# Key sums of linear attention turned round on column tiles, with GpSimd summing z and new constants for the kernel's planner

## The chip, the cores and the metric

The kernel runs on one NeuronCore of a Trainium2 chip. The metric is the device time of one execution in microseconds (us); lower is better. The names of the engines in the profile are PE (TensorE, matmuls), PEld (its weight loads), DVE (VectorE), ACT (ScalarE), POOL (GpSimd) and SP (the engine that issues nearly all DMAs).

## The reference

Random-feature attention over 8 batches, 8 heads, 576 positions and 64 dimensions, followed by a two-layer feed-forward block with softplus on the 4608 tokens:

```python
def phi(x):
    proj = np.einsum('bhsd,md->bhsm', x, omega)
    sq = np.sum(x * x, axis=-1, keepdims=True) / 2.0
    h = proj - sq
    h = h - np.max(h, axis=-1, keepdims=True)
    return np.exp(h) / np.sqrt(m)
q_p, k_p = (phi(q_s), phi(k_s))
kv = np.einsum('bhsm,bhsd->bhmd', k_p, v)
z = np.sum(k_p, axis=2)
num = np.einsum('bhsm,bhmd->bhsd', q_p, kv)
den = np.einsum('bhsm,bhm->bhs', q_p, z)[..., None] + 1e-06
x = (num / den)                # tokens x 512
h = x @ w_in                   # 512 x 2048
g = np.maximum(h, 0.0) + np.log1p(np.exp(-np.abs(h)))
out = g @ w_out                # 2048 x 512
```

There are 128 features. All is float32; the feed-forward products are made of three fp32r products each (high x high, high x low, low x high).

## The kernel before

**Units.** Attention is worked in *quads*: four heads of one batch, two quads a batch, 16 in all. A quad has five units `u` for keys (tile names in `k`) and five for queries (`q`): four of 128 positions and a last one with the remaining 64. A unit is loaded, its squares are summed, its rows are projected on omega (`project`, line 445 for batches 0 and 1, line 588 from batch 2 on), and the features are the exponentials (`ph`), 128 of them for four heads side by side. Batch 0 ("early") has its own path.

**Key sums.** For keys of batch 1 on, `plan_sums` makes kv and z on TensorE: `outer` (line 676) multiplies features (weights, 128 positions x 128 features) by V with a 65th column of ones (128 x 65, 4 heads one after the other), so column 64 of each head is z. Units 0 to 2 go into one sum, units 3 and 4 into a second; `part` (ScalarE) keeps the first aside in `kvp`, `whole` (VectorE) adds the second to it and gives `kvs`; `z`, `z_turn`, `out_z` and `in_z` turn z by a VectorE transpose, send it out in 4 stores and read it back broadcast to all partitions (`zb`). Query features are divided by their denominator (VectorE reduction `den`, line 784; the division itself mostly on GpSimd, line 794), turned through DRAM (`qdq`) and multiplied by `kvs` (`num`, lines 954, 997 and 1048), which gives the columns of x. There the weights are 128 x 64, so the two heads of a pair stand in two column tiles of the array, side by side.

**Feed-forward.** Blocks of 512 tokens (the first two of 256) run through 16 slices of 128 hidden units: `layer1` (lines 1412 to 1414), softplus on ScalarE and VectorE, `layer2` (lines 1441 to 1443). The last two blocks are joined in `plan_pair` (lines 1199 and 1256 to 1258), seven products in place of eight. Each weight slice is 512 KB, packed, and is opened by five steps in `plan_weights`: lowest bits (line 333 on ScalarE, 335 on VectorE), `rebias`, `joined`, `high_part`, `low_part`.

**What sets the order.** Each piece of work is a `Work` with a due time and a cost for each engine that can do it. `in_order` plays these through and takes, on the engine that is free first, the startable work that is due first; the program is written out in that order, and every engine runs its instructions in it. Costs (`act`, `dve`, `pool`, `dma` and numbers beside each `do`) and due times (offsets from `due`, and the tables `KEYS`, `QUERIES`, `IN`, `OUT`) are constants. `with_fill` puts matmuls of no use ("fillers", line 1571, weights `ident` or `idle`) where the play leaves TensorE idle in its first part, to keep its clock up. Work that uses the port shared by VectorE and GpSimd is kept apart by added waits.

## Time and profile before

| what | value |
|---|---|
| three runs, median | 996.35 us (996.18 to 997.45) |
| span of the profiled execution | 995.2 us |
| TensorE busy | 989.6 us (99%) |
| VectorE, ScalarE, GpSimd busy | 783.6, 722.7, 206.4 us |
| granted TensorE clock, mean | 1.000 |
| transfers, whole span | 124.49 MB, 125 GB/s |

The span goes from the first to the last instruction of the profiled execution; the runs' own times lie 1.15 us above it in the median. A busy TensorE in this table is one on which some matmul is in flight; matmuls overlap, so the price of one is read from the starts of its neighbours, not from its duration. An fp32 product shows as two records, an fp32r product or a transpose as one.

### The profile page before, as it was taken

What the parts mean: (1) busy time and instruction counts of PE and PEld (TensorE: products, weight loads), DVE (VectorE), ACT (ScalarE), POOL (GpSimd) and SP (SyncE); (2) the same over time, 40 slices, a digit from 0 to 9 for tenths busy, and PEclk for the clock granted to TensorE, in tenths of its full rate; (3) what the DMA queues carried; (4) which work ended last, traced back from release to release, by engine and by line L of the source; (5) the groups of instructions that cost most, each with busy time, mean ns of one, the idle gap of its engine ahead of it and who ended that gap; (6) DMA issues with size and microseconds to landing.
All of it is one profiled execution on the core that took longest, in us unless ns stands there. A gap on an engine that the chain in (4) does not pass through costs nothing.

```text
span 995.2 us, 17488 instructions
## 1 busy us (share of the span) xinstructions
PE 989.6 (99%) x5495; PEld 830.9 (83%) x5495; DVE 783.6 (79%) x2306; ACT 722.7 (73%) x1794; POOL 206.4 (21%) x235
## 2 busy tenths in 40 slices
PE   9999999999999999999999999999999999999998
PEld 8988888888888888888878888888888878888886
DVE  6899986889898888888879886887787958676620
ACT  7999887879777777877777776776776656666520
POOL 3313232312221122101212121112011214223000
PEclk9999999999999999999999999999999999999999
DMA  9982355454464455543454444434542331000011
GB/s 321 352 282 90 111 162 152 138 160 141 136 183 139 125 138 160 159 128 113 138 144 133 123 129 119 155 106 113 138 141 75 80 92 43 0 1 1 1 43 42
DMA packets 117628, 124.49 MB, mean 125 GB/s; under 512 B 16288, under 2 KB 93728, under 8 KB 117536
## 3 DMA queue, kind: packets, MB, share of 16 engines
q1 hardware_dynamic: 117392, 123.26, 41.4%
q8 instruction: 43, 0.70, 0.3%
q14 instruction: 49, 0.40, 0.1%
q10 hardware_dynamic: 144, 0.13, 0.0%
HBM read 97.37 MB, written 25.98 MB: 124 GB/s over the span
## 4 chain that ended last, share of the span: by engine, by line
PE 98%; DVE 1%; ACT 0%; issue 0%
PE banks L1441 11%; PE banks L1412 11%; PE banks L1442 10%; PE banks L1443 10%; PE banks L1413 10%; PE banks L1414 10%; PE banks L1199 8%; PE banks L676 5%; PE banks L588 5%; PE banks L1256 3%; PE banks L1258 3%; PE banks L1257 3%; PE banks L445 2%; PE banks L997 2%; PE banks L735 1%; PE banks L954 1%
## 5 line engine op out<-in xcount | busy, mean ns | idle before, releaser
L1412 PE MATMUL banks<-xh,wi 128*128 128x512 f32 (+1 forms) x512 | 188.8, 369 | 0.4 <-DVE u L1427 0.4
L1413 PE MATMUL banks<-xl,wi 128*128 128x512 f32 (+1 forms) x512 | 186.1, 363 | 0.0
L1414 PE MATMUL banks<-xh,wi 128*128 128x512 f32 (+1 forms) x512 | 185.9, 363 | 0.0
L1441 PE MATMUL banks<-wo,gh 128*128 128x512 f32 x448 | 178.6, 399 | 0.0
L1442 PE MATMUL banks<-wo,gh 128*128 128x512 f32 x448 | 175.5, 392 | 0.0
L1443 PE MATMUL banks<-wo,gl 128*128 128x512 f32 x448 | 175.0, 391 | 0.0
L1418 ACT ACTIVATE u<-banks 128x512 f32<-128x512 f32 (+1 forms) x128 | 70.1, 548 | 73.4 <-PE banks L1414 60.5
L1412 PEld LDWEIGHTS banks<-xh,wi 128*128 128x128 f32 x512 | 96.4, 188 | 17.2 <-issue 1.2
L1414 PEld LDWEIGHTS banks<-xh,wi 128*128 128x128 f32 x512 | 96.4, 188 | 15.6
L1413 PEld LDWEIGHTS banks<-xl,wi 128*128 128x128 f32 x512 | 96.6, 189 | 13.9
L1441 PEld LDWEIGHTS banks<-wo,gh 128*128 128x128 f32 x448 | 84.2, 188 | 18.5 <-issue 4.3
L1443 PEld LDWEIGHTS banks<-wo,gl 128*128 128x128 f32 x448 | 84.1, 188 | 18.5
L1442 PEld LDWEIGHTS banks<-wo,gh 128*128 128x128 f32 x448 | 84.4, 188 | 13.3
L1427 DVE SCALAR_TENSOR_TENSOR u<-banks,u 128x512 f32<-128x512 f32 (+1 forms) x128 | 78.4, 613 | 15.8 <-ACT u L1424 15.4
L612 ACT ACTIVATE phq<-phq,smq 128x128 f32<-128x128 f32 x216 | 71.8, 395 | 14.7 <-DVE smq L608 14.7
L794 POOL TENSOR_TENSOR phq<-phq,dnq 128x512 f32<-128x512 f32 (+1 forms) x46 | 41.9, 911 | 189.2 <-DVE dnq L790 113.1
L612 ACT ACTIVATE phk<-phk,smk 128x128 f32<-128x128 f32 x216 | 71.9, 397 | 10.7 <-DVE smk L608 10.7
L784 DVE CUSTOM_DVE_ANT_0 restq<-phq,zb 128x128 f32<-128x128 f32 x280 | 72.7, 293 | 4.8 <-ACT phq L612 4.0
L1421 ACT ACTIVATE u<-u 128x512 f32<-128x512 f32 (+1 forms) x128 | 74.4, 581 | 1.8
L1424 ACT ACTIVATE u<-u 128x512 f32<-128x512 f32 (+1 forms) x128 | 74.6, 584 | 1.3
L1431 ACT CAST gh<-u 128x512 fp32r<-128x512 f32 (+1 forms) x97 | 55.8, 576 | 18.0 <-PE banks L1442 17.1
L1435 POOL TENSOR_TENSOR gl<-u,gh 128x512 fp32r<-128x512 f32 (+1 forms) x41 | 45.1, 1101 | 106.4 <-ACT gh L1431 31.5
(224 smaller groups left out, 2097.3 us busy)
## 6 DMA issues: line engine op xcount, KB each, us to landing
xk<-ky SPq DMA_DIRECT2D x48, 384.0 KB
xq<-qy SPq DMA_DIRECT2D x48, 384.0 KB
qdq<-restq SPq DMA_DIRECT2D x56, 256.0 KB
out<-o SPq DMA_DIRECT2D x36, 256.0 KB
vk<-vv SPq DMA_DIRECT2D x70, 130.0 KB
rawi<-wi SPq DMA_DIRECT2D x16, 512.0 KB
rawo<-wo SPq DMA_DIRECT2D x16, 512.0 KB
q<-qdq SPq DMA_DIRECT2D x64, 128.0 KB
```

The source lines that it names most:

```text
L612: nc.scalar.activation(b["ph"][:, c], b["ph"][:, c], AF.Exp, bias=b["sm"][:, 2, c : c + 1])
L784: i = nc.vector.tensor_tensor_reduce(jk[r, c], ph[r, c], q.zb[r, h], 1.0, 1e-6, ALU.mult, ALU.add, dn[r, 0, c : c + 1])
L1199: nc.tensor.matmul(b[key], x, y, start=fresh and not kk and not n, stop=kk == 1 and n == 2, skip_group_check=True)
L1412: nc.tensor.matmul(b["h"], wh, xh[:, cc, t], start=cc == 0, stop=False)
L1413: nc.tensor.matmul(b["h"], wh, xl[:, cc, t], start=False, stop=False)
L1414: nc.tensor.matmul(b["h"], wl, xh[:, cc, t], start=False, stop=cc == NCC - 1)
L1421: nc.scalar.activation(b["u"], b["u"], AF.Exp, scale=-1.0)
L1424: nc.scalar.activation(b["u"], b["u"], AF.Ln, bias=1.0)
L1427: nc.vector.scalar_tensor_tensor(b["u"], b["h"], 0.0, b["u"], ALU.max, ALU.add)
L1441: nc.tensor.matmul(acc[tt], gh, w2[fc][:, 0], start=fc == 0, stop=False)
L1442: nc.tensor.matmul(acc[tt], gh, w2[fc][:, 1], start=False, stop=False)
L1443: nc.tensor.matmul(acc[tt], gl, w2[fc][:, 0], start=False, stop=fc == NFC - 1)
```

## The change

1. `outer` is turned: V is the weights (128 positions x 64), the features stream (128 columns). The two heads `j` of a pair write to the two halves of the partitions, in two column tiles. The sums come out as dimension by feature and are turned back by two transposes (`kv_turn`) and a copy (`kv_turned`). V loses its column of ones (260 columns become 256) and its loads for the remainder have 128.
2. z: in batch 1 four more products per unit (line 732 of the changed kernel), ones as weights of 32 columns. From batch 2 on `plan_z` sums the features of the five units on GpSimd, and `kv_turn` adds the positions up with four products of ones by that sum. The row goes out in one store in place of four.
3. GpSimd may do `low_bits`.
4. x pieces of 257 to 320 tokens are read and multiplied as 256 and the rest, not as one.
5. The planner: new costs, all due times new, a buffer can have several users (`uses`), weight loads stand behind the first K load, the rounding of units is kept in order.

```diff
@@ plan_weights
-                return nc.vector.tensor_scalar(low.bitcast(I32), low, 2.0**-29, 7.0, ALU.mult, ALU.min)
+                engine = nc.vector if e == "DVE" else nc.gpsimd
+                return engine.tensor_scalar(low.bitcast(I32), low, 2.0**-29, 7.0, ALU.mult, ALU.min)
...
-        a = do(("ACT", "DVE"), (aw + 0.03, dw2), due + 3.12, low_bits, after=[l], port=True)
+        a = do(("ACT", "DVE", "POOL"), (aw + 0.03, dw2, pw), due + 60.24, low_bits, after=[l], port=True)
@@ new function
+    def plan_z(q, b, i, u, due, es):
+        if q.b < 2:
+            return
...
+        def add():
+            add_ = nc.gpsimd.tensor_tensor
+            x = b["ph", i]
+            if u == 1:
+                q.z = at.tile([P, 4, M], F32, name=f"z{q.nm}", tag=q.z_slots["z"], bufs=1)
+                b0, i0, _ = q.z_first
+                return add_(q.z, b0["ph", i0], x, ALU.add)
+            if u < 4:
+                return add_(q.z, q.z, x, ALU.add)
+            for j in (1, 0):
+                r, h = slice(j * D, (j + 1) * D), slice(2 * j, 2 * j + 2)
+                a_ = add_(q.z[r, h], q.z[r, h], x[r, :2], ALU.add)
+            return a_
@@ plan_sums
-            for c in range(4 if u < 4 else 2):
-                end = k == len(keys) - 1 and c == (3 if u < 4 else 1)
-                cs = slice(c, c + 1) if u < 4 else slice(c, 4, 2)
-                nc.tensor.matmul(kv[:, cs], ph[:, c], v[:, cs], start=not k and not c, stop=end, skip_group_check=True)
+            end = k == len(keys) - 1
+            for p in range(2):
+                for j in range(2):
+                    r, c = (slice(0, P), 2 * j + p) if u < 4 else (slice(j * D, (j + 1) * D), p)
+                    nc.tensor.matmul(
+                        kv[j * D : (j + 1) * D, p], v[r, c], ph[r, c], start=not k and not p, stop=end, skip_group_check=True
+                    )
+            for c in range(4 if na > 2 else 0):
+                nc.tensor.matmul(
+                    kv[32 * c : 32 * (c + 1), 2], (ones if u < 4 else halves[:, c // 2 : c // 2 + 1]).broadcast_to([P, 32]),
+                    ph[:, c if u < 4 else c % 2], start=False, stop=end, skip_group_check=True,
+                )
...
+        def kv_turn():
+            y["turned"] = y["bank"][:, 2 * M if na < 3 else 0 :][:, : 2 * M].rearrange("p (a m) -> p a m", m=P)
+            for p in range(2):
+                nc.tensor.transpose(y["turned"][:, p], q.kvp[:, p], ident)
+            for c in range(0 if na > 2 else 4):
+                nc.tensor.matmul(
+                    y["bank"][32 * c : 32 * (c + 1), :M], ones.broadcast_to([P, 32]), q.z[:, c], start=True, stop=True,
+                    skip_group_check=True,
+                )
...
         def out_z():
-            q.zd = dram.tile([4, P], F32, name=f"zd{q.nm}", tag="zd", bufs=2)
-            for i in range(4):
-                r = slice(i * 32, (i + 1) * 32)
-                nc.sync.dma_start(q.zd[:, r], q.zr[i * 32 : i * 32 + 4])
+            q.zd = dram.tile([4, M], F32, name=f"zd{q.nm}", tag="zd", bufs=2)
+            nc.sync.dma_start(q.zd, q.z[::32, 0] if na < 3 else q.kvp[::32, 2])
...
-                "PE", 0.86 if u < 4 else 0.43, due - 235.34, lambda k=k: outer(k), after=[m] if k else [x for x, _ in deps],
+                "PE", (0.50 if u < 4 else 0.31) + 0.30 * (na - 2) + (0 if k else 0.10), due - 315.31, lambda k=k: outer(k), after=[m] if k else [x for x, _ in deps],
@@ plan_queries
-            sizes = [w] if w <= 320 else [256, w - 256]
+            sizes = [w] if w <= 256 else [256, w - 256]
@@ one of the due tables
-IN = (-77.35, -86.63, -115.20, 17.77, 69.89, -10.45, 6.40, 31.06, 149.98, 21.85, 124.48, 208.49, 408.59, 38.21, 62.49, 277.15)
+IN = (-75.17, 72.61, -490.00, 27.33, 179.69, -137.36, 49.07, 85.61, 200.71, 247.20, 129.07, 95.05, 245.06, 123.50, 329.19, -78.28)
```

What moves, at three places.

The queue of loads (SP) at the very start, before (`omf_76` is omega, `rawi` and `rawo` are weight slices of 512 KB, `xk_0_1` to `xk_0_4` and `x_first` key units of batch 0):

```order
L241 DMA omf_76<-om 128x128
L324 DMA rawi_115<-wi 128x1024
L413 DMA xk_0_1_117<-k 128x2x260
L505 DMA x_first<-k 128x260
L413 DMA xk_0_2_121<-k 128x2x260
L413 DMA xk_0_3_123<-k 128x2x260
```

One weight slice stands ahead of the key units. The same place in the changed kernel:

```order
L247 DMA omf_76<-om 128x128
L331 DMA rawo_118<-wo 128x1024
L331 DMA rawi_120<-wi 128x1024
L331 DMA rawo_122<-wo 128x1024
L422 DMA xk_0_1_124<-k 128x2x260
L331 DMA rawo_126<-wo 128x1024
L422 DMA xk_0_2_129<-k 128x2x260
L518 DMA x_first<-k 128x260
L422 DMA xk_0_3_132<-k 128x2x260
```

Three slices stand ahead of `xk_0_1` and a fourth ahead of `xk_0_2`; the second half of `x_first` (130 KB) went behind `xk_0_2`.

TensorE's queue at the same time, before (projections of key units, and fillers with `ident`):

```order
L445 MATMUL banks<-omf,x_first 128x128 x4
L457 MATMUL banks<-small,x_first 128x56 x4
L1571 MATMUL banks<-ident 128x512
L445 MATMUL banks<-omf,xk_0_1_117 128x128 x4
L457 MATMUL banks<-small,xk_0_1_117 128x56 x4
L1571 MATMUL banks<-ident 128x512
L445 MATMUL banks<-omf,xk_0_2_121 128x128 x4
L457 MATMUL banks<-small,xk_0_2_121 128x56 x4
```

One filler stands ahead of each. And in the changed kernel:

```order
L455 MATMUL banks<-omf,x_first 128x128 x4
L467 MATMUL banks<-small,x_first 128x56 x4
L1649 MATMUL banks<-ident 128x512 x7
L455 MATMUL banks<-omf,xk_0_1_124 128x128 x4
L467 MATMUL banks<-small,xk_0_1_124 128x56 x4
L1649 MATMUL banks<-ident 128x512 x3
L455 MATMUL banks<-omf,xk_0_2_129 128x128 x4
L467 MATMUL banks<-small,xk_0_2_129 128x56 x4
```

Seven fillers and three; over the whole program the fillers with `ident` go from 9 (groups of 1, 1, 2, 3, 1, 1) to 23 (7, 3, 2, 1, 1, 1, 7, 1).

TensorE's queue where a quad's second key sum ends, before (third batch; `tq` are rounded query rows for a projection):

```order
L1414 MATMUL banks<-xh,wi_1119 128x512
L676 MATMUL banks<-vk_0_3_3287,phk_0_3_3402 128x65 x4
L676 MATMUL banks<-vk_0_4_3374,phk_0_4_3486 128x2x65 x2
L588 MATMUL banks<-oms,tq_1_4_3484 128x256 x2
L1412 MATMUL banks<-xh,wi_1119 128x512
```

The sum is complete there. The same quad in the changed kernel:

```order
L1521 MATMUL banks<-wo_246,gl_10_3575 128x512
L728 MATMUL banks<-phk_0_3_3463,vk_0_3_3323 64x128 x4
L728 MATMUL banks<-phk_0_4_3547,vk_0_4_3453 64x128 x4
L1490 MATMUL banks<-xh,wi_1101 128x512
L1491 MATMUL banks<-xl,wi_1101 128x512
L1492 MATMUL banks<-xh,wi_1101 128x512
L1490 MATMUL banks<-xh,wi_1101 128x512
L1491 MATMUL banks<-xl,wi_1101 128x512
L1492 MATMUL banks<-xh,wi_1101 128x512
L749 MATMUL banks<-ident,kvp_0_3424 128x128 x2
L751 MATMUL banks<-z_0_3301,small 32x128 x4
```

Six other products stand between the sum and its turning (6 to 13 rows over the 14 quads, 6 or 7 rows in seven of them and 9 in one).

## Rows read from the trace of the kernel before

**Rows 1.** The page: busy us of each engine (parts 1 and 4)

```profile
PE 989.6 (99%) x5495; PEld 830.9 (83%) x5495; DVE 783.6 (79%) x2306; ACT 722.7 (73%) x1794; POOL 206.4 (21%) x235
...
PE 98%; DVE 1%; ACT 0%; issue 0%
```

**Rows 2.** All waits of PE: who waited for whom, us, times, longest

```profile
PE banks L1571 <- DVE small L263: 1.1, 1, 1.1
PE banks L1412 <- DVE u L1427: 0.4, 1, 0.4
PE banks L877 <- DVE xl L931: 0.3, 1, 0.3
```

**Rows 3.** Timeline, PE's last matmul: start us, duration us, instruction

```profile
990.98 0.39 PE L1258 MATMUL banks<-wo,wi 128*128 128x512 f32 x1
```

**Rows 4.** Timeline of PE round a first key sum

```profile
443.81 0.39 PE L1413 MATMUL banks<-xl,wi 128*128 128x512 f32 x1
444.03 0.39 PE L1414 MATMUL banks<-xh,wi 128*128 128x512 f32 x1
444.26 2.79 PE L676 MATMUL banks<-vk,phk 128*128 128x65 f32 x24
...
447.17 0.40 PE L1442 MATMUL banks<-wo,gh 128*128 128x512 f32 x1
```

**Rows 5.** Timeline of PE round a second key sum

```profile
467.12 0.40 PE L1443 MATMUL banks<-wo,gl 128*128 128x512 f32 x1
467.36 1.50 PE L676 MATMUL banks<-vk,phk 128*128 128x65 f32 x12
...
468.93 0.40 PE L1442 MATMUL banks<-wo,gh 128*128 128x512 f32 x1
```

**Rows 6.** Timeline of PE round an x product of 128 columns

```profile
668.90 0.39 PE L1443 MATMUL banks<-wo,gl 128*128 128x512 f32 x1
669.22 1.09 PE L954 MATMUL banks<-q,kvs 128*64 128x128 f32 x16
...
670.58 0.40 PE L1442 MATMUL banks<-wo,gh 128*128 128x512 f32 x1
```

**Rows 7.** Timeline of PE round an x product of 64 columns

```profile
792.39 0.39 PE L1414 MATMUL banks<-xh,wi 128*128 128x512 f32 x1
792.71 0.69 PE L954 MATMUL banks<-q,kvs 128*64 128x64 f32 x16
...
793.66 0.39 PE L1413 MATMUL banks<-xl,wi 128*128 128x512 f32 x1
```

**Rows 8.** Timeline of PE, two transposes and what follows

```profile
52.30 0.39 PE L868 MATMUL banks<-ident,xq 128*128 128x128 f32 x2
52.53 0.61 PE L877 MATMUL banks<-kvs,xq 128*128 128x130 f32 x4
```

**Rows 9.** Timeline of PE at the start, fillers and projections

```profile
7.02 0.50 PE L1571 MATMUL banks<-ident 128*128 128x512 f32 x1
7.46 0.72 PE L445 MATMUL banks<-omf,xk 64*128 64x128 f32 x8
...
8.91 0.72 PE L445 MATMUL banks<-omf,xk 64*128 64x128 f32 x8
...
13.10 0.96 PE L1571 MATMUL banks<-ident 128*128 128x512 f32 x3
13.99 0.71 PE L445 MATMUL banks<-omf,xk 64*128 64x128 f32 x8
```

**Rows 10.** Windows: engines busy, clock, DMA share, GB/s in 5 to 10 us

```profile
5.00:10.00 5.00, 5.00 (x54) 3.78 (x54) 3.01 (x8) 2.54 (x6) 2.13 (x3) 1.00 1.06 346
```

**Rows 11.** Timeline of ACT: squares of the second key unit

```profile
6.38 0.42 ACT L426 ACTIVATE xk<-xk 128x256 f32<-128x256 f32 x1 [0.69 <-DMA xk<-k]
```

**Rows 12.** Groups of POOL by form: count, busy us, mean ns, idle before

```profile
L1435 POOL TENSOR_TENSOR gl<-u,gh 128x512 fp32r<-128x512 f32 x27 | 34.9, 1291 | 66.4 <-ACT gh L1431 17.9 <-DVE gh L1431 10.7 <-PE banks L588 9.7
L1326 POOL TENSOR_TENSOR R<-R,f 128x256 f32<-128x256 f32 x8 | 5.9, 743 | 28.6 <-DVE R L1316 28.3
```

More of the change, by code (lines that the diff above doesn't have):

```diff
@@ L171, in in_order @@
         for box, key in w.give:
-            free[box[key]] = w.done, e
-            held[box[key]][-1][1::2] = w.done + lag(e, "PE"), len(out)
+            left, last = shared.get((id(box), key), (box.get(("uses", key), 1), (0.0, e)))
+            left, last = shared[id(box), key] = left - 1, max(last, (w.done, e))
+            assert left >= 0, key
+            if left:
+                continue
+            free[box[key]] = last
+            held[box[key]][-1][1::2] = last[0] + lag(e, "PE"), len(out)
         can.remove(w)
@@ L254, in favor_softplus_kernel @@
     make_identity(nc, eye)
+    for i in range(4):
+        at.tile([P, 3, 8], F32, name=f"sm{i}", tag=f"sm.{i}", bufs=1)
+    at.tile([P, 16], F32, name="gap1")
     nc.gpsimd.tensor_copy(dense, eye)
@@ L260, in favor_softplus_kernel @@
     halves, ones = small[:, :2], small[:, 2:3]
+    for i in range(4):
+        const.tile([P, 4, 4], F32, name=f"dn{i}", tag=f"dn.{i}", bufs=1)
     xh = const.tile([P, NCC, RING], F32R, name="xh")
@@ L614, in plan_split @@
         ld = do(
-            "SP", read(n * (P + D) * P * 4), due - 89.77, load, behind=prev.get("load"), take=[("x", b, "x")],
+            "SP", read(n * (P + D) * P * 4), due - 19.07, load, behind=prev.get("load"), take=[("x", b, "x")],
         )
@@ L828, in plan_queries @@
         d = do(
-            "DVE", 0.87, due + 46.98, den, after=es + [q.zc], steps=4, soon={es[1]: 0.62} if q.b > 1 and u < 4 else {},
+            "DVE", 0.87, due + 203.77, den, after=es + [q.zc], steps=4, soon={es[1]: 0.62} if q.b > 1 and u < 4 else {},
             take=[("dn", b, "dns"), ("ph", bu, ("rest", first))],
@@ L933, in plan_early_x @@
         t = do(
-            "PE", 0.45 if tail else 0.46, due - 227.12, turn, after=[d for _, d in rows], heat=1024, behind=prev.get("turn_x"),
+            "PE", 0.45 if tail else 0.46, due - 250.22, turn, after=[d for _, d in rows], heat=1024, behind=prev.get("turn_x"),
             take=[("any", y, "b")], give=[(b, "x") for b, _ in rows],
@@ L1349, in plan_pair @@
-            q2 = do(*dp(2 * P), sdue - 139.44, lambda e, b=b: sums(e, 2, b), after=[q1, f1], port=True)
-            q3 = do(*dp(2 * P), sdue - 44.26, lambda e, b=b: sums(e, 3, b), after=[q2], give=[(b, ("tag", "f2"))], port=True)
-            q4 = do(*dp(2 * P), sdue - 32.45, lambda e, b=b: sums(e, 4, b), after=[q2], port=True)
+            sdue = due - 14.77
+            f1 = do(*dp(TB), sdue + 351.37, lambda e, b=b, j=j, nm=nm: whole(e, b, "f1", j, nm), after=gate + [done_w["i", j]], take=[("two", b, ("tag", "f1"))], port=True, behind=pe.get((5, j - 2)))
@@ new lines, in plan_pair @@
+            f2 = do(*dp(TB), sdue + 28.20, lambda e, b=b, j=j, nm=nm: whole(e, b, "f2", j + H, nm), after=gate + [done_w["i", j + H]], take=[("two", b, ("tag", "f2"))], port=True, behind=f1)
+            q1 = do(*dp(2 * P), sdue + 129.40, lambda e, b=b, nm=nm: sum1(e, b, nm), after=[f2], take=[("two", b, ("tag", "R"))], port=True)
+            q2 = do(*dp(2 * P), sdue - 229.25, lambda e, b=b: sums(e, 2, b), after=[q1, f1], port=True)
+            q3 = do(*dp(2 * P), sdue + 226.78, lambda e, b=b: sums(e, 3, b), after=[q2], give=[(b, ("tag", "f2"))], port=True)
@@ new lines, in plan_pair @@
+            p7 = prod(7, "C", True, due - 24.83, [l34] + late["done"][3], kind=hp, give=tg)
+            s7 = do(*cp, due + 11.37, lambda e, b=b, nm=nm: copied(e, b, "C", "s7", nm), after=[p7], take=[("two", b, ("tag", "s7"))])
+            p5 = prod(5, "A", False, due - 40.15, [s2] + late["done"][1], give=[(b, ("tag", "L"))])
+            c22 = do("DVE", dve(TB), due - 322.32, lambda b=b: added(b["s7"], b["A"], b["s7"]), after=[p5, s7])
+            p4 = prod(4, "C", False, due - 338.85, [s7] + late["done"][4])
@@ L1481, in store @@
                 nc.sync.dma_start(out[t0 + tt * P : t0 + (tt + 1) * P, :], o["t"])
[L1483 to L1485 removed]
+            a = do("DVE", 0.34, due + 216.43, left, after=[ends[tt]], take=[("ph" if last else "t2", o, "s")])
+            r = do("ACT", 0.27, due - 19.52, right, after=[ends[tt]] if last and tt == n // P - 1 else [a], give=[(box, ("acc", i, tt))])
+            do("SP", dma(0.25, 0.8, 1.05), due + 45.94, store, after=[a, r], give=[(o, "s")], late=LATE["store"])
     assert NQ == 2
```

329 lines of the change are left out of this document (175 added, 154 removed).

## The prediction

> **What bounds the kernel now.** I read the page first: TensorE is busy for 989.6 of the 995.2 us and holds 98% of the chain that ended last [rows 1]. The view of waits says the same from the other side: after its start TensorE waits twice for anything, 0.4 and 0.3 us [rows 2]. So the span is a row of matmuls without holes, plus some 4 us behind the last one, which starts at 990.98 [rows 3]. The order at the end (last product, two copies, a store) is alike in both kernels, so that tail stays. What the change is worth is then a sum over TensorE alone: what its queue holds less, what it holds more, and every wait that is new. VectorE (79%) and ScalarE (73%) [rows 1] may lose or gain work without any effect until TensorE waits for them.
>
> A matmul's duration in a row is its latency; its price is the distance to the next start. Two 512-column products stand 0.23 us apart (443.81, 444.03, 444.26) [rows 4]. So I price a group of other matmuls, a **visit**, by starts: start of the second product behind it, less start of the last one ahead, less two spacings of 0.228. An fp32 product is two records in these rows.
>
> **The key sums, quads of batches 2 to 7 (12 quads).** Before, a visit for three units (24 records of 65 columns) costs 447.17 - 444.03 - 0.456 = 2.68 us [rows 4], and that for the last two (12 records) 468.93 - 467.12 - 0.456 = 1.35 [rows 5]. The new form has 64 columns of V as weights and 128 feature columns streaming, two heads side by side in two column tiles. Its nearest rows are the x products from kvs, the same shape of tile: 16 records of 128 columns cost 670.58 - 668.90 - 0.456 = 1.22 us [rows 6], 16 of 64 columns 793.66 - 792.39 - 0.456 = 0.81 [rows 7]. The difference gives 0.41/16 = 0.0257 us for each record and 64 columns; what is left, 0.40 us, is the fixed cost of going into the tiled form and out again. The first visit (24 records of 128) is then 0.40 + 24 x 0.0513 = 1.63: 1.05 us less. The second has 16 records, 8 of them in 64 x 64 tiles, which no row shows: 1.02 if those run at the narrow price, 1.22 if like the others, 1.42 if the change of tile shape in the middle costs half a fixed cost; I take 1.12, between the first two, since they keep the same two tiles side by side: 0.23 less. Added is the turning: two transposes, 0.23 for two (52.30 to 52.53) [rows 8], and the row of ones against z, 8 records in four tiles of 32 columns: 0.40 + 8 x 0.0257 = 0.61 if four run side by side where two did (0.81 if only two do; 0.21 if the fixed cost is not paid again). So 0.84 us more. Per quad 1.05 + 0.23 - 0.84 = 0.44 saved, **-5.3 us** for twelve (bounds: 11.3 saved to 0.7 lost).
>
> **The key sums of batch 1 (2 quads)** keep z on TensorE: 5 times 8 records more in 32-column tiles, 1.03 us per quad at 0.0257, two transposes 0.23, visits of 1.63 and 1.12: 4.01 against 2.68 + 1.35 = 4.03 before. But each unit goes from 64- to 32-column tiles and back, 8 changes within the visits. A change is worth 0 to 0.2 us (half of the fixed 0.40); I take the middle, 0.8 a quad: **+1.6 us** (0 to 3.2).
>
> **The x products** lose their 320-column form for 256 + 64: by the same prices 0.40 + 8 x 5 x 0.0257 either way, nothing.
>
> **The first 55 us.** The counts of the queue say that 14 more filler matmuls stand there (23 against 9, in groups of 7, 3, 2, 1, 1, 1, 7, 1). Fillers wait for nothing but are paid: one alone stands for 7.02 to 7.46, three for 13.10 to 13.99, so 0.225 each more [rows 9]; 14 x 0.225 = 3.2. Against that, three fewer visits of the row-tiled projections (24 against 27) at 0.40: -1.2. Together **+2.0 us**.
> The queue of loads explains the fillers. Ahead of the second K tile (xk_0_1) now stand three weight loads instead of one, ahead of the third four. Each is 512 KB; in 5 to 10 us the transfers ran at 346 GB/s [rows 10], so 1.5 us each. xk_0_1, whose squares ScalarE began at 6.38 [rows 11] and whose projection began at 7.46 [rows 9], comes 3.0 us later, at 10.5 or up to 0.5 sooner (squares take 0.42); the 7 fillers end at about 8.8, so TensorE waits 1.2 to 1.7 there. For xk_0_2, projected at 8.91 [rows 9], three more weights less the 130 KB of x_first that now stand behind it are 4.2 us: 13.1 against 12.4, when TensorE would come to it, so 0 to 0.7 more. I take **+1.5 us** for both (0 to 3).
>
> **Other engines.** GpSimd gets the sums of z (36 of 512 elements, 24 of 256), most of the remainders of the projections, and the lowest three bits of 6 of 32 weights; it was 21% busy. A 512-element subtraction takes 1.29 us there and a 256-element one 0.74 [rows 12]. I price this at nothing: TensorE has 6 or more rows of other work between the last outer product and the turning. If the cover is gone, see the third rival. The bits are six operations off TensorE's path; whether GpSimd does them or not moves nothing I can see. The new due times and costs move every engine's order; where TensorE's row stays full, that is free, and the old row was full [rows 2].
>
> **Sum.** -5.3 + 1.6 + 2.0 + 1.5 = -0.2 us on a span of 995.2. The median of the runs (996.35) lies 1.15 us above the profiled span, and I carry that over: 996.35 - 0.2 = **996.2 us**. About 0.2% (2 us) is what a measurement can tell here from no change: 994.4 to 998.3 is "same".
>
> **Rivals.**
> First, faster: the tiled forms are cheap next to each other. Then batch 1's changes cost 0, the second visit 1.02, so 0.54 saved in each of twelve quads (6.5 us), and the early loads land nearly in time (0.5): -6.5 + 0 + 2.0 + 0.5 = -4.0, 992.4 us. For it: within a visit the records of the two tiles keep their pace whatever their number [rows 6, 7]. Against: no row has two tile shapes next to each other. Chance 0.28.
> Second, slower: every change of tile shape pays. The rows show that going from the full array into column tiles and out costs 0.40 [rows 6, 7]. Then the second visit is 1.42 and a quad saves 1.05 - 0.07 - 0.84 = 0.14 (1.7 us in all), batch 1 loses 3.2: -1.7 + 3.2 + 2.0 + 1.5 = +5.0, 1001.3 us. It decides as soon as a change costs over 0.15 us. The Trainium skill has this as a rule, in "TensorEngine Tiling (Array Packing)", section "Tiling Modes", Key Properties: changing the tiling mode, not just the tile, drains TensorE; the fixed cost in rows 6 and 7 agrees for full array to tiles, and no row here shows tile to tile. Chance 0.14.
> Third, slower: GpSimd's sums become the wait. The turning needs z complete. In the quads where six 512-column products (6 x 0.228 = 1.4 us) stand between, the sum over unit 3 (1.29) and the two over unit 4 (2 x 0.74) take 2.8 us behind unit 3's exponentials, while TensorE reaches the turning about 1.1 + 1.4 = 2.5 us after them: 0.3 us late, more when a subtraction stands ahead in GpSimd's queue. Behind the waiting transposes TensorE's whole row stands. Eight of the fourteen quads have such a short cover; at 0.4 each that is 3.2 us, 999.4 us. It decides where GpSimd begins over 0.3 us late. For it: GpSimd loses its idle time; against: its share was 21%, and TensorE waits for GpSimd nowhere before [rows 2]. Chance 0.14.
>
> **How the numbers follow.** The sum has 0.44. Faster 0.28, within 0.2% 0.44, slower 0.28. The range is from 991.5 to 1001.3: it reaches the first rival's time with a little of the lower bound of the turning, and the second's time; what is below (all lower bounds at once) and above (rivals two and three together) is some 2 in 10.
>
> **What would show it.** In the changed profile: 24-record visits of the outer product at 1.6 us by starts, second visits near 1.1, turning near 0.84; in batch 1 whether each unit costs 0.65 or 1.0; TensorE's waits by line: at the projections of xk_0_1 and xk_0_2 before 14 us if the loads are late, and none at the transposes of kvp unless GpSimd is late. I am wrong if the key sums save under 2 or over 8 us, or if TensorE waits over 3 us after the head.

## The result and the profile after

The changed kernel takes **1007.69 us** (median of 4 runs, 1006.32 to 1010.54), the kernel before 996.66 (996.18 to 997.45) beside it: ratio 1.0113, interval 1.0101 to 1.0126. It is 1.1% slower. The forecast was 996.2, the range ended at 1001.3. The profiled run of the changed kernel took 1006.32 us, its span is 1004.5 (995.2 before).

The page, its busy times and chain, answering [rows 1]:

```profile
PE 994.2 (99%) x5801; PEld 815.4 (81%) x5801; DVE 795.4 (79%) x2303; ACT 708.9 (71%) x1778; POOL 305.7 (30%) x310
...
PE 96%; DVE 1%; DMA 1%; ACT 0%; SPq 0%; issue 0%; POOL 0%; DVEq 0%; ACTq 0%
```

TensorE is still the bound. All its waits, answering [rows 2] (who waited for whom; us, times, longest):

```profile
PE banks L996 <- DVE xq L969: 1.6, 1, 1.6
PE banks L1334 <- ACT o L1556: 1.6, 1, 1.6
PE banks L1649 <- DVE small L274: 1.1, 1, 1.1
PE banks L455 <- DMA xk<-k: 0.6, 1, 0.6
PE banks L455 <- DVE xq L969: 0.6, 1, 0.6
PE banks L1490 <- DVE u L1505: 0.4, 1, 0.4
```

Four are new, and none stands at the transposes of kvp (L749). Its last matmul, answering [rows 3], starts 8.73 us later; behind it come 4.8 us instead of 4.2:

```profile
999.71 0.39 PE L1336 MATMUL banks<-wo,wi 128*128 128x512 f32 x1
```

The key sums of a quad of batches 2 to 7, timelines of TensorE round its first visit, its second and its turn, answering [rows 4, 5]:

```profile
406.07 0.40 PE L1521 MATMUL banks<-wo,gl 128*128 128x512 f32 x1
406.40 1.53 PE L728 MATMUL banks<-phk,vk 128*64 128x128 f32 x24
...
408.19 0.40 PE L1491 MATMUL banks<-xl,wi 128*128 128x512 f32 x1
...
430.23 0.40 PE L1521 MATMUL banks<-wo,gl 128*128 128x512 f32 x1
430.56 1.24 PE L728 MATMUL banks<-phk,vk 128*64 128x128 f32 x16
...
432.06 0.39 PE L1520 MATMUL banks<-wo,gh 128*128 128x512 f32 x1
...
433.68 0.39 PE L1521 MATMUL banks<-wo,gl 128*128 128x512 f32 x1
433.91 0.38 PE L749 MATMUL banks<-ident,kvp 128*128 128x128 f32 x2
434.22 0.42 PE L751 MATMUL banks<-z,small 128*32 128x128 f32 x8
...
434.91 0.39 PE L1491 MATMUL banks<-xl,wi 128*128 128x512 f32 x1
```

By starts, less two spacings of 0.228, these are 1.66, 1.37 and 0.77 us: 3.81 a quad against 4.03 before. In batch 1 the three units of a first visit go to and fro between tiles of 64 and of 32 columns:

```profile
69.14 0.28 PE L1492 MATMUL banks<-xh,wi 128*128 128x256 f32 x1
69.34 0.66 PE L728 MATMUL banks<-phk,vk 128*64 128x128 f32 x8
69.93 0.42 PE L732 MATMUL banks<-phk,small 128*32 128x128 f32 x8
70.29 0.66 PE L728 MATMUL banks<-phk,vk 128*64 128x128 f32 x8
...
72.51 0.40 PE L1520 MATMUL banks<-wo,gh 128*128 128x512 f32 x1
```

That visit costs 3.02 (with one spacing of 0.119 for the 256-column product ahead), the second 2.08, the two transposes 0.22: 5.32 against 4.02. So twelve quads save 2.6 us and two lose 2.6. **Summed over all visits the key sums cost 56.4 us; before, 56.5.** What the change was made of moves nothing; the 8.7 us are elsewhere.

Where: I took every matmul's distance to the next start, less the median of its form in the kernel before. Up to 66 us TensorE lost 8.6 us that way where it lost 6.1 before, and its fillers stand for 12.1 instead of 7.6: about **6.9 us in the head**. Between 830 and 860 us 1.7 more are lost than before. Behind 860 the changed kernel gains 0.7. That leaves 0.8 for the stretch from 66 to 830 us, by difference.

The head, TensorE at the start, answering [rows 9] (there the projection of the second K tile starts at 7.46):

```profile
7.06 1.90 PE L1649 MATMUL banks<-ident 128*128 128x512 f32 x7
9.59 0.71 PE L455 MATMUL banks<-omf,xk 64*128 64x128 f32 x8 [0.62 <-DMA xk<-k]
```

The first product of layer 1, timelines of TensorE before and now:

```profile
53.33 0.37 PE L1412 MATMUL banks<-xh,wi 128*128 128x256 f32 x1
...
57.12 0.36 PE L1490 MATMUL banks<-xh,wi 128*128 128x256 f32 x1
```

These times differ from run to run. In seven traces with this head (the changed kernel's two and five of the kernels below) the second projection starts between 8.86 and 10.18 us and layer 1 between 56.01 and 57.74; of the kernel before there is one trace.

In between ScalarE had nothing to spare. It was busy 18.68 us of the stretch from 20 to 40 before, and now for all of it (windows, before and now: us, then busy us of PE, PEld, DVE, ACT and POOL with their instructions, the granted clock PEclk, the DMA share, GB/s):

```profile
20.00:40.00 20.00, 20.00 (x226) 18.48 (x225) 15.77 (x49) 18.68 (x54) 5.88 (x7) 1.00 1.01 384
...
20.00:40.00 20.00, 20.00 (x220) 18.60 (x219) 17.49 (x52) 20.00 (x61) 9.14 (x8) 1.00 1.02 399
```

By 54 us it had done 22 `rebias` steps (one for each weight slice that is opened), against 12.

The wait at 64 us, timeline of GpSimd, VectorE and TensorE:

```profile
60.69 3.79 POOL L361 TENSOR_TENSOR wi<-rawi,wi 128x512 fp32r<-128x512 f32 x3
...
63.22 1.28 DVE L961 TENSOR_TENSOR dnq<-dnq,small 128x4 f32<-128x4 f32 x1
...
65.28 0.66 PE L996 MATMUL banks<-stack,xq 128*128 128x64 f32 x4 [1.59 <-DVE xq L969]
```

A VectorE operation on four elements a row takes 1.28 us; it starts with the third GpSimd operation (63.20 to 64.48) and ends with it, at 64.50. Its twin in the kernel before takes 0.16. The Trainium skill has a rule for this in "GPSIMD Engine Reference", section "Specifications" (GpSimd's memory interfaces are shared with VectorE, which contends with two SBUF inputs), and in "SBUF — State Buffer", section "Terms" (the loser waits for the whole instruction); the rows agree.

The wait at 842 us, timeline of VectorE and TensorE: an output copy stands behind the store that still reads its buffer, and TensorE behind the copies (in brackets the idle time ahead and what ended it).

```profile
838.42 0.42 DVE L1553 COPY o<-banks 128x256 f32<-128x256 f32 x1 [1.74 <-PE banks L1521]
843.15 0.42 DVE L1553 COPY o<-banks 128x256 f32<-128x256 f32 x1 [4.30 <-DMA out<-o]
...
844.03 0.50 PE L1334 MATMUL banks<-wo,gh 128*128 128x512 f32 x1 [1.56 <-ACT o L1556]
```

The four output tiles of that block share one buffer. The first store landed after 2.04 us, the second after 3.74. Its 16 parts tell why: 15 of them landed within 2.02 us, at 841.31, and the last at 843.03. A packet of 16 KB that loads instructions was in flight from 840.28 to 841.71, and the last eight packets of the store ran one after another from 841.70 on (DMA queues from 839.9 to 843.1 us: packets, MB, share of the 16 engines):

```profile
q8 instruction: 1, 0.02, 2.8%
```

So two things make this wait: the shared buffer, and a load of instructions that meets the store on its way.

### The profile page after: what moved, and what is told of

Same layout as the page of the kernel before. It is cut to its first block, busy times and chain, and to the rows that moved or that the text cites. A ratio compares the mean times of both kernels' runs of the same rounds, so it can differ in the third digit from the quotient of the medians.

```text
span 1004.5 us, 18184 instructions
## 1 busy us (share of the span) xinstructions
PE 994.2 (99%) x5801; PEld 815.4 (81%) x5801; DVE 795.4 (79%) x2303; ACT 708.9 (71%) x1778; POOL 305.7 (30%) x310
## 4 chain that ended last, share of the span: by engine, by line
PE 96%; DVE 1%; DMA 1%; ACT 0%; SPq 0%; issue 0%; POOL 0%; DVEq 0%; ACTq 0%
PE banks L1490 11%; PE banks L1519 11%; PE banks L1491 10%; PE banks L1520 10%; PE banks L1492 10%; PE banks L1521 10%; PE banks L1277 7%; PE banks L601 5%; PE banks L728 4%; PE banks L1334 3%; PE banks L1336 3%; PE banks L1335 3%; PE banks L455 2%; PE banks L1075 2%; PE banks L1032 1%; PE banks L811 1%
## 5 line engine op out<-in xcount | busy, mean ns | idle before, releaser
L1490 PE MATMUL banks<-xh,wi 128*128 128x512 f32 (+1 forms) x512 | 191.3, 374 | 0.4 <-DVE u L1505 0.4
L1490 PEld LDWEIGHTS banks<-xh,wi 128*128 128x128 f32 x512 | 96.4, 188 | 23.3 <-issue 5.2
L860 DVE CUSTOM_DVE_ANT_0 restq<-phq,zb 128x128 f32<-128x128 f32 x280 | 75.1, 303 | 10.7 <-ACT phq L625 7.2
L1513 DVE TENSOR_TENSOR gl<-u,gh 128x512 fp32r<-128x512 f32 (+1 forms) x100 | 68.6, 686 | 12.9 <-ACT gh L1509 12.2
L1509 ACT CAST gh<-u 128x512 fp32r<-128x512 f32 (+1 forms) x100 | 56.5, 565 | 29.2 <-PE banks L1520 24.5
L595 POOL TENSOR_TENSOR tq<-xq,tq 64x512 fp32r<-64x512 f32 (+1 forms) x45 | 52.1, 1157 | 79.3 <-DVE gl L1513 21.1
```

Of the source, the lines that this page charges most:

```text
L860: i = nc.vector.tensor_tensor_reduce(jk[r, c], ph[r, c], q.zb[r, h], 1.0 / M if q.b > 1 else 1.0, 1e-6, ALU.mult, ALU.add, dn[r, 0, c : c + 1]
L1490: nc.tensor.matmul(b["h"], wh, xh[:, cc, t], start=cc == 0, stop=False)
```

## The experiments

**The changed kernel once more**, beside other runs of the same kind.

> The changed kernel as it is, for a yardstick on the chip that runs the next three. My account of its loss (span 1004.5 against 995.2): about 7 us are lost before 66 us of the span (14 fillers x 0.225 = 3.2, new waits 2.1, the rest in matmuls of another shape between), batch 1's key sums cost 2.6 us more, those of batches 2 to 7 2.6 less, one wait of 1.6 us at 842. Expected: 1006 to 1009 us, ratio to before 1.010 to 1.013, granted clock at least 0.996. Rival: the loss is the chip's, a lower clock in the changed kernel: then the clock lies under 0.99 or the ratio moves by more than 0.003 on another chip.

1008.78 us, ratio 1.0116 (1.0099 to 1.0132). The same waits are there, the one at 842 us with 2.3 us, and behind it the granted clock fell, which no run of the kernel before shows (window; PEclk, the third number from the end, is the mean over the stretch; 0.50 is 1.2 GHz):

```profile
845.00:850.00 5.00, 4.80 (x14) 3.80 (x15) 1.59 (x3) 1.53 (x4) 0.00 (x0) 0.66 0.14 52
```

At 0.66 instead of 1.00 these 5 us do some 1.7 us less work (an estimate: 0.34 x 5). It happens in some runs and not in others; the runs of the changed kernel spread over 4 us, those of before over 1.

**The ones of batch 1 last.** All 64-column tiles of a visit first, then all ones of it, so a unit changes the tile no more.

```
-            for c in range(4 if na > 2 else 0):
+            for b_, i_, u_ in keys if end and na > 2 else []:
+                for c in range(4):
...
-                    ph[:, c if u < 4 else c % 2], start=False, stop=end, ...
+                        b_["ph", i_][:, c if u_ < 4 else c % 2], start=False, ...
```

> The changed kernel with the products of ones of batch 1 (z) not behind each unit but together behind the last unit of each key sum: the same products, but 2 changes of tile shape in place of 6 in the first sum of a quad and 3 in place of 4 in the second. Theory, that each change of shape costs 0.15 us (0.20 to the next start instead of 0.05): visits of about 2.4 instead of 3.02 and 1.95 instead of 2.08 us, 1.5 us less over the two quads. Rival, that the products of ones cost what they cost wherever they stand: visits as in the changed kernel, within 0.1 us.

The visits take 2.45 (from the rows) and 1.94 us, against 3.02 and 2.08:

```profile
69.41 0.28 PE L1493 MATMUL banks<-xh,wi 128*128 128x256 f32 x1
69.62 1.53 PE L728 MATMUL banks<-phk,vk 128*64 128x128 f32 x24
71.08 0.86 PE L733 MATMUL banks<-phk,small 128*32 128x128 f32 x24
...
72.21 0.39 PE L1521 MATMUL banks<-wo,gh 128*128 128x512 f32 x1
```

Four changes fewer in the first visit are 0.57 us, so **one change of tile shape costs 0.14 to 0.15 us**. The whole time, 1008.36 (ratio 1.0101, 1.0083 to 1.0120), doesn't show the 1.4 us of both quads against the 4 us that the runs spread.

**One shape.** The remainder's V is filled with zeros to 128 rows, as the kernel before had it, so no visit has a tile of 64 rows.

```
-                    r, c = (slice(0, P), 2 * j + p) if u < 4 else (slice(j * D, (j + 1) * D), p)
+                    r, c, cp = slice(0, P), 2 * j + p, 2 * j + p if u < 4 else p
...
-        "vv": np.concatenate(_rows(v[1:]), axis=3),
+        "vv": _rows_apart(v[1:]),
```

> The changed kernel with V of the remainder padded with zeros (as the kernel before had it), so that the fifth unit's outer products stand in the same two column tiles of 128 rows as the fourth's: the second visit of a quad has no change of tile shape any more (batch 1: 2 fewer... its ones still stand between). Same order. Theory, a change of tile shape costs 0.15 us: second visits of batches 2 to 7 at 1.22 instead of 1.37 us, 12 x 0.15 = 1.8 us less in all; batch 1 unchanged. Rival, that the change in the middle costs nothing and the 0.15 us are the 64-row form's own: 1.37 us as before.

The second visit goes from 1.37 to 1.22 us in each of the twelve quads:

```profile
430.35 0.40 PE L1520 MATMUL banks<-wo,gl 128*128 128x512 f32 x1
430.68 1.09 PE L727 MATMUL banks<-phk,vk 128*64 128x128 f32 x16
...
432.05 0.40 PE L1519 MATMUL banks<-wo,gh 128*128 128x512 f32 x1
```

Tiles of 128 and of 64 rows next to each other are a change of shape as well. That the 64-row form isn't dear by itself shows in batch 1: there the ones between the units change the shape in any case, and its second visits cost 2.08 us with 64 rows and with 128. The time is 1008.34, ratio 1.0112 (1.0085 to 1.0139); its profiled run has a clock of 0.66 at 65 to 70 us.

**A buffer of its own for the second output** at 840 us, and, in another kernel, **the third of GpSimd's three operations at 61 us given to VectorE**, behind the small one.

```
+                apart = i == len(sizes) - 3 and tt == 1
+                o["t"] = (at if last or apart else ff).tile([P, DM], F32, name=f"o_{i}_{tt}", tag="zb.1" if apart else o["s"], bufs=1)
```

```
+    plan[401].engine = "DVE"
+    plan.insert(403, plan.pop(401))
```

> The changed kernel, but the second output tile of the last single block has a buffer of its own instead of the one that all four share, so that the third copy need not wait for the store of the second. Theory, that this one wait (1.6 us in one trace, 2.3 in another, after which the granted clock fell to 0.66 in 845 to 850 us) is both a part of the loss and the reason why the changed kernel's runs scatter over 4 us: wait under 0.3 us, clock 1.00 there, median 2 to 4 us less than the changed kernel's 1008.8 in the same session, and the runs within 2 us. Rival, that the copies wait for the tile's products, not for the store: wait and scatter stay.

> The changed kernel with one weight slice's last opening step (the third of three that stand back to back on GpSimd at 60.7 to 64.5 us) on VectorE instead, behind the query's division there. In the changed kernel a product of 128 x 4 on VectorE, at 63.22, takes 1.28 us while that step runs on GpSimd (0.16 in the kernel before), and TensorE waits 1.6 us at 64 for what follows. Theory, that the two engines share a port and GpSimd held it: the product takes 0.16 to 0.2 us, TensorE's wait at 64 falls to 0.6 us or less and the clock no longer falls in 65 to 70 us in any profile: 1 us less, more where the clock had fallen. Rival, that VectorE's queue is simply full there: the wait stays over 1.2 us.

The first: 1005.26 us, ratio 1.0089 (1.0068 to 1.0110); the wait at L1334 is gone (the products there start at 842.13 and 842.36), though the second store landed late once more, after 4.03 us, and the clock of the profiled run is 1.000. One of its four runs still took 1009.42 us at a mean clock of 0.993, so this wait isn't all of the scatter.

The ten other kernels that keep the changed order and the shared buffer show the other half of the cause. In seven of them the second store landed after 3.8 to 4.4 us, and TensorE waited 1.6 to 2.3 us, each time 2.2 less than the landing. In one it landed after 2.43 and the wait was 0.3; in one the third store was the late one (3.42, a wait of 0.65). In the last, the one with all K tiles first below, the packet of instructions had passed before the second store's data moved: the four stores landed within 2.04 us, and TensorE waited for none.

The second: 1007.16, ratio 1.0107 (1.0091 to 1.0123); the small operation takes 0.16 us again (timeline), and TensorE's wait is 0.5 instead of 1.6 (waits):

```profile
63.17 0.16 DVE L961 TENSOR_TENSOR dnq<-dnq,small 128x4 f32<-128x4 f32 x1
```

```profile
PE banks L996 <- DVE xq L969: 0.5, 1, 0.5
```

Both causes are shown by the waits. The whole time tells neither from the changed kernel's (1.0101 to 1.0126), and in the second kernel waits at L1490 of 1.7 us in all stand in place of 0.4.

**The four together.**

> Four edits of the earlier runs together in the changed kernel's order: ones last in batch 1, one tile shape in the second sums, the output tile with a buffer of its own, the step moved from GpSimd to VectorE. If the parts add up and nothing else comes late: 1.4 + 1.8 + 1.6 + 1.0 us off a span of 1004.5 without a fall of the clock, 998.7, a time of about 1000.3, still some 3 us over the kernel before, all of it from the first 66 us; runs within 2 us, clock 1.00. Rival, that another wait takes the place of the mended ones: 1003 us or more.

1003.75 us, ratio 1.0073 (1.0058 to 1.0088), span 1001.6. Of the span 2.9 us come back where 5.8 were expected, of the median time 3.9; 7.1 stay. The visits sum to 53.5 us here, 2.9 less. The rival's time came: in this trace the second K tile's wait is 1.1 us instead of 0.6, the waits at L1490 are 1.0 instead of 0.4, and two of 0.5 to 0.6 us are new.

**The head.** Five kernels move its loads, fillers and weight steps. Fewer fillers (groups of 7, 3 and 7 cut to 1):

> The changed kernel with 1, 1 and 1 fillers in place of the groups of 7, 3 and 7 (at 8, 11 and 49 us); nothing else. Theory, that the first two groups only stand where TensorE would wait for the late K tiles: the second projection stays at 9.6, the third moves by at most 0.4 us, the group at 49 gives back up to 1.3 us unless its projection waits for its data: together 0 to 1.7 us less than the changed kernel. Rival, that fillers are a cost by themselves: 14 x 0.225 = 3.2 us less. Second rival: TensorE's clock falls when it idles at 8 us, and the kernel is over 1 us slower than the changed one, with a granted clock under 1 in the first 20 us.

1007.85, ratio 1.0112 (1.0094 to 1.0130): nothing in the whole time. The time of the fillers turns into the wait for the K tile that they stood in (timeline); but TensorE then ran at the low clock (window), so what the fillers would give back at the full clock isn't shown:

```profile
8.43 0.83 PE L455 MATMUL banks<-omf,xk 64*128 64x128 f32 x8 [1.32 <-DMA xk<-k]
```

```profile
10.00:15.00 5.00, 5.00 (x29) 4.24 (x31) 3.85 (x10) 4.61 (x14) 0.40 (x1) 0.50 1.09 355
```

Loads of the early weights behind the K tiles, their steps spread out:

> The changed kernel with one weight slice ahead of the K tiles instead of three, as in the kernel before: the other three early slices are loaded behind the second, third and fourth K tile and their opening steps stand behind the K tiles' squares on ScalarE and VectorE; the first two groups of fillers (7 and 3) become 1 and 1. The rest of the order is untouched. Theory, that the early slices hold up the head: squares of the second K tile at about 6.4 instead of 9.57, its projection at about 7.1 instead of 9.59, the wait for it (0.6) gone, and TensorE 2.4 us ahead to the end: 1004 to 1005.5 us. Rival, that ScalarE (busy for all of 20 to 40 us) sets the head: the second projection is early all the same, but TensorE waits for exponentials later, the first product of layer 1 stays at 56.5 to 57.5, and the time is that of the changed kernel within 0.7 us.

1011.8, ratio 1.0143. The second tile's projection starts at 7.06, but by 16 us TensorE waits for exponentials, 3.9 us in two waits (timeline of the longer), and then runs at the low clock (window):

```profile
16.77 0.48 PE L455 MATMUL banks<-omf,xk 64*128 64x128 f32 x2 [2.29 <-ACT xk L505]
```

```profile
20.00:25.00 5.00, 5.00 (x33) 4.57 (x33) 2.37 (x7) 4.39 (x16) 0.66 (x2) 0.50 0.99 390
```

Weight steps on ScalarE later (21 steps put back), then loads and steps both, then the same with fillers enough to keep TensorE busy:

> The changed kernel, with the first opening step of 15 weight slices (rebias on ScalarE, 0.7 us each), which stands up to 160 pieces of work ahead of the step that needs it, moved to just ahead of that step, and the three first steps of the two last slices moved behind the head. Until the first product of layer 1 ScalarE then has 9 such steps less. Theory, that the opening of weights too early on ScalarE and VectorE (22 rebias and 16 joined by 54 us, against 12 and 9 before) holds up the head: first product of layer 1 at 54 to 55.5 instead of 57.1 to 57.3 us, 1.5 to 3 us less in all. Rival, that TensorE's own queue (fillers, visits) sets the head: first product within 0.5 us of 57.1. Second rival, that it is given back behind 57 us, where ScalarE is busy too: first product early, the 96th within 0.7 us of the changed kernel's 92.6.

> As the run with the keys first (one weight slice ahead of the K tiles, 1 and 1 fillers for 7 and 3), but now the opening steps of the other three early slices stand behind the first projections' exponentials on ScalarE and VectorE (some 8 to 12 us later than in the changed kernel) instead of among them. In the run with the keys first those steps stood in ScalarE's queue ahead of the exponentials at 13 to 18 us, TensorE waited 3.9 us for these and its clock fell to half. Theory, that slices opened too early, by their loads and by their steps together, cost the head: the 77th projection at 12.5 to 14 us instead of 17.5, no wait for exponentials over 0.5 us, first product of layer 1 at 53.5 to 55.5 instead of 56 to 57.3, the time 1.5 to 3.5 us less than the changed kernel. Rival, that the work is only moved to where ScalarE is full: first product of layer 1 within 0.7 us, or the 96th at 91.5 to 93 us as in the changed kernel.

> Third try at the head of the changed kernel: all K tiles and the first queries loaded ahead of the three early weight slices (the two tries before held up either the exponentials or the queries' loads, and TensorE's clock fell to half), their opening steps behind the first exponentials, 1 and 1 fillers in place of 7 and 3, but 6, 3 and 3 in place of 2, 1 and 1 in the next groups, so that TensorE idles less at 13 to 25 us. Theory, that the early slices cost the head: 77th projection at 12.5 to 14 us, clock over 0.9 in 15 to 30 us, first product of layer 1 at 53.5 to 55.5 us and the time 1.5 to 3.5 us less than the changed kernel. Rival, that ScalarE and VectorE have the same work before the first product in any order: it stays at 56 to 58 us.

1012.7, 1011.4 and 1007.38 us (ratios 1.0162, 1.0151, 1.0111). With the steps put back layer 1's first product comes at 55.65, little below the 56.01 to 57.74 of the unchanged head, and its 97th product at 95.59 (92.58 in the changed kernel): more than it gained is given back. With loads and steps both, the 77th projection (counted in records of L455 and L467) comes at 13.53 instead of 17.50, as my theory said, and then ScalarE waits 2.5 us for a tile of queries, TensorE 2.6 behind it, and the clock falls to 0.50. With fillers the clock stays at 1.00, the 77th projection comes at 15.60, and layer 1 starts at 57.99. So **none of these moves brings the head's lost time back**; the theory that they could fell each time. Two of the tries lost time to the clock as well, so they don't show that no move could. The reverse was left to try: the kernel before with its second to fourth weight load ahead of the K tiles (two more ahead of the second, a third ahead of the third), and its fillers there raised to 7 and 3.

```
+    for at_, n_ in {17: 7, 25: 3}.items():
+        plan[at_] = (*plan[at_][:2], n_)
+    moves = {59: 2.1, 65: 2.2, 88: 4.5}
```

> The reverse, on the kernel before: its second, third and fourth weight slice are loaded ahead of the second and third K tile as in the changed kernel, with 7 and 3 fillers in place of the first two single ones; nothing else is moved, and the opening steps stay where they are. Theory, that K tiles which land 4 to 5 us late set the whole head back: second projection at 9 to 10 instead of 7.46 us, the 77th at 16 to 18 instead of 12.27, first product of layer 1 at 55.5 to 58 instead of 53.3, and the time 2.5 to 5 us over the kernel before. Rival, that the slack of the head takes it: first product within 1 us of 53.3 and the time within 1 us of the kernel before.

1000.84 us, ratio 1.0043 (1.0028 to 1.0058), the profiled run at a clock of 1.000: **the early loads, with the fillers that go with them, cost the kernel before about 4 us** (2.8 to 5.8). Its second K tile comes late in the same way (timeline of ScalarE, its squares at 8.70 for 6.38 [rows 11]); its projection starts right behind the fillers, and for the third tile TensorE waits:

```profile
8.70 0.42 ACT L426 ACTIVATE xk<-xk 128x256 f32<-128x256 f32 x1 [3.09 <-DMA xk<-k]
...
8.72 0.72 PE L445 MATMUL banks<-omf,xk 64*128 64x128 f32 x8
...
11.14 0.71 PE L445 MATMUL banks<-omf,xk 64*128 64x128 f32 x8 [0.42 <-DMA xk<-k]
```

Layer 1 starts at 55.99 (2.7 later), and the last matmul 3.9 later.

**The bits on VectorE** instead of GpSimd, all of them:

> The changed kernel with the lowest three bits of the six slices that GpSimd had on VectorE, in the same places of the order. On GpSimd one took 2.01 us, on VectorE 0.43; in the trace of the changed kernel VectorE waits for GpSimd's at 58.16 (0.91 us), and the chain of waits runs through one at 38.8 to 40.9. Theory, that GpSimd's bits are on the path of the head: first product of layer 1 0.7 to 1.5 us earlier than 57.1, the time 0.5 to 1.5 us less. Rival, as I predicted, that they move nothing: within 0.4 us at the first product.

1009.15, ratio 1.0118 (1.0098 to 1.0137): nothing that shows. Layer 1 starts at 55.94, but so it does in the two kernels above that leave the bits alone and were run beside it (56.01 and 56.30). An operation takes 2.0 us on GpSimd and 0.42 on VectorE.

**The key sums alone.** The kernel before, its order kept, with only the turned sums put where the old ones stood (it leaves out the factor 1/128 of z); and then without GpSimd's sums (the products with ones read a tile of ones, so z isn't computed at all).

> The kernel before with its own order of loads, steps, fillers, bits and output buffers; only the key sums of batches 1 to 7 are the turned ones, put at the places where the old ones stood: V stays, the exponentials stream, the remainder runs over all 128 rows (its V is zero where another head's rows lie, so no tile is 64 rows high), the sums of the exponentials are made by GpSimd for all fourteen, the two transposes and the four products with ones stand two PE steps behind the second visit, and ScalarE copies both out. It takes 0.97 KB less for other buffers, none of which is on the path. Theory (the key sums alone were worth something; the head and a store's buffer cost the change its time): the visits take 1.66 + 1.22 + 0.78 = 3.66 us of PE instead of 4.03 for each of fourteen quads, 5.2 us in all, the head stays where before has it (first product of layer 1 at 53.3, last product at about 986), about 991.5 in all, ratio 0.995. Rival (turned sums gain nothing anywhere, since the added turn waits for the copy and its rows hold up what follows, or GpSimd's sums make VectorE late): 996.7 or more, ratio 1.000 or above.

> The kernel of the run before, in the order of before, with the turned products but without the 70 sums of exponentials on GpSimd: the products with ones read a tile that holds ones from the start, so its denominators are not the reference's (in the run before they lacked the factor 1/128). It tells apart what made the run before 30 us slower. Theory (GpSimd's sums hold the buffers of the key exponentials and share VectorE's port, so the exponentials and the products behind them come late, in an order that was planned without them): without them the waits of TensorE shrink from 24 us to a few, and the visits are worth their 5.2 us: 992 to 997. Rival (the turn and its two copies on ScalarE, put in where the order leaves no room, are what is late): the time stays at 1015 to 1027, with the waits on the copies of the turned sums and of their row.

1026.57 us (ratio 1.0311, 1.0288 to 1.0335) and 1003.05 (1.0072, 1.0048 to 1.0096). In the second the visits cost 51.6 us, 4.9 less than before (5.2 expected), and still its last matmul starts 4.0 us later. The waits of TensorE, the two longest of the first kernel:

```profile
PE banks L1517 <- DVE u L1532: 4.6, 3, 3.7
PE banks L684 <- DVE phq L601: 3.4, 2, 2.3
```

and the longest three of the second:

```profile
PE banks L1515 <- DVE u L1530: 1.7, 2, 1.4
PE banks L1057 <- DVE phk L603: 1.6, 1, 1.6
PE banks L594 <- ACT zs L724: 1.4, 6, 0.2
```

My theory fell as to the time, and held for the visits. GpSimd's sums cost 23.5 us in an order that doesn't know them, in part through the clock (0.83 of full speed over 60 to 70 us, 0.89 over 105 to 120, 0.83 over 435 to 445). Without them 8.9 us are still lost beside the visits. 5.6 of these are new waits of TensorE, 1.6 for the copy of z's row and 0.7 for that of the first sum among them; some 3 are not traced. So the turned sums, put in without moving anything else, lose more than their visits save. In the changed order, which is made with them, TensorE waits for none of them; what such an order would give without the changed head no run shows.

## Why the prediction was wrong, point by point

- **Key sums of batches 2 to 7: forecast -5.3, came -2.6.** The first visit (1.63 against 1.66) and the turn (0.84 against 0.77) were near. The step that failed is the second visit. Of 1.02, 1.22 and 1.42 the prediction says "I take 1.12, between the first two, since they keep the same two tiles side by side": it came to 1.37, close to the third. The tiles stay, but their height changes from 128 to 64 rows, and that is paid like any other change of shape: 1.22 without it.
- **Batch 1: forecast +1.6, came +2.6.** "A change is worth 0 to 0.2 us ... I take the middle": it is worth 0.14 to 0.15, so eight are 1.2 a quad where 0.8 was taken; the rest is that the second visit's records cost 1.22 without any change, not 1.12.
- So the second rival had the mechanism of these two terms, every change of shape pays, at too high a price (0.2 a change; it said +1.5 together, the forecast -3.7, and it came to 0.0), and the first was wrong. The Trainium skill's rule that stood beside it ("TensorEngine Tiling (Array Packing)", section "Tiling Modes", Key Properties: a change of the tiling mode drains TensorE) agrees with the rows, tile to tile as well. The sign that I had named for being wrong, key sums that save under 2 us, came.
- **The head: forecast +3.5, came to about +6.9.** The cause was named rightly (weight loads ahead of the K tiles, late by one to three transfers) and the wait for the second tile was seen where it was forecast. Two steps failed. "Fillers wait for nothing but are paid" counted 14 x 0.225 apart from the wait; they stand in it, as the kernel with fewer of them shows (six fillers less, a wait of 1.32 in their place). And I stopped at the two tiles: what comes late there goes on through the projections (17th at 9.59 for 7.46, 77th at 17.50 for 12.27) to layer 1, 3.8 us late. The kernel before with early loads, and little else moved, shows about 4 us of it.
- The step **"where TensorE's row stays full, that is free, and the old row was full"** failed outright. A full row of before says nothing of the new order. Two waits of 1.6 us came from it, one by GpSimd's work beside VectorE's, one by a buffer that four outputs share when a load of instructions held up one of their stores. Neither was in the sum, nor was what the clock loses behind them in some runs.
- **Right:** the x products, nearly (320 columns against 256 + 64: 0.06 us more each); the bits, which move nothing that shows; GpSimd's sums in the changed order, in time everywhere, so the third rival was false (though GpSimd does weigh on VectorE at 64 us); and the tail, within 0.6 us.
- The sum as it came: key sums -0.1, head +6.9, the wait at 842 us +1.7, behind 860 us -0.7, the rest by difference +0.9, which no run traced (the x products are 0.5 of it): +8.7 at the last matmul. The tail adds 0.6 to the span (9.3 in all). The time outside the span is about 1.8 us in every run of both kernels, and the median of the changed kernel lies 1.4 above its profiled run, which had no fall of the clock up to its last matmul.
- **Open:** of the 7 us that stay with all four mends the early loads would account for about 4, if they cost in the changed order what they cost in the old one; that isn't shown, since no move in the changed order gave it back. The rest is spread over the head and over short waits, and no run isolated it.

## What to carry to other kernels

Price a change of order by a part of its own: read what each queue carries ahead of the first tile that TensorE waits for, follow that delay through the projections to the main product, and don't add fillers to a wait in which they stand. Price tiles by their number of changes of shape, rows included, and put equal shapes together. Where a buffer is shared by several stores, count with the slowest part of a store, not with its usual landing. A saving that is real on the bounding engine's rows may still not be had by putting it into an order made without it.

## What the hardware showed that I had not expected

- A change of tile shape costs TensorE 0.14 to 0.15 us whether columns (64 to 32) or rows (128 to 64) change.
- A VectorE operation on 128x4 elements took 1.28 us instead of 0.16 beside a GpSimd operation of 1.28 us, and 0.16 again when that operation was gone.
- A single wait in an otherwise full row can cost the clock. Behind waits of 2.3 us at 845 (the changed kernel once more) and of 1.58 at 64 (the kernel with one shape) the granted clock was 0.66 over the next stretch, 845 to 850 and 65 to 70 us; behind waits of 1.56 and 1.59 at the same two places (the changed kernel's first trace) it was 1.00.
- Two stores of the same size, 3 us apart, landed after 2.04 and 3.74 us. 15 of the second one's 16 parts were as quick as the first; the last eight packets of the sixteenth ran behind a 16 KB packet of instructions, and TensorE waited 1.6 us for them.
